# Attention and a mixture of soft slots on one core: q and k of four heads turned together, and combine's weights repeated for four results

## The chip, the cores and the metric

One Trainium2 chip, of which the kernel uses one core. The metric is the device time of one execution in microseconds (us). Three runs of the kernel before gave 297.88, 295.6 and 296.4 us; their median is 296.4. A profile was taken of one more execution, and all durations in this text come from it.

The engines by their names in the profile: PE is the matrix engine (PEld its weight loads), DVE the vector engine, ACT the scalar engine, POOL the general one, SP the one that here only issues transfers. POOL works through its instructions in order, and a transfer that it issues is one of them.

## The reference

Inputs: q, k, v of 8 batches, 12 heads, 448 tokens, 64 wide; phi (768 x 32); w1 and w2 of 8 experts (768 x 1024, 1024 x 768).

```python
scores = scale * np.matmul(q, k.transpose(0, 1, 3, 2))
m = np.max(scores, axis=-1, keepdims=True)
e = np.exp(scores - m)
attn = e / (np.sum(e, axis=-1, keepdims=True) + np.exp(-m) + 1e-09)
x = np.matmul(attn, v)             # then (batch * token, head * width) = 3584 x 768
...
logits = x @ phi
d = softmax of logits over the 3584 rows;  slot_input = d.T @ x
slot_out = relu(slot_input @ w1) @ w2        # four slots for each of the eight experts
c = softmax of logits over the 32 slots;   out = c @ slot_out
```

## The kernel before, in words

**Pairs and slots.** The 96 heads (8 batches of 12) are worked off as 48 pairs, six to a batch. `for s in range(3, NPAIR + 1)` (L769) goes over slots; a slot has two half-steps y = 0 and 1, and `hs = 2 * s + y` counts them. Slots 0 to 2 are written out by hand in `ramp` (L726). For slots 3 to 41 the work of each half-step is a string of words in `order` (L698), six rows, one for each value of s % 6. Slots 42 to 48 have no table.

**The words.** `T` turns q and k of pair s + 6: 28 transposes of 64x64 blocks on PE (L256, 7 token blocks, two heads, q and k), the two heads in two corners of the array, into one PSUM tile of 128x896, which one copy brings to SBUF (`T`, L241; on ACT in the ramp and for two of six pairs behind it, else on DVE). `B0` to `B3` (`Bk`, L352) make the scores of pair s, transposed, in four blocks of keys; a second matmul adds the negative row maxima, and ACT takes the exponential. Between them stand the score matmuls of a pair some three further on (`A`, L274), for the row maxima on DVE; the letters behind B give the order of these six matmuls. `V0` to `V3` and `H` (`AV`, L418) multiply by v; `H` does the last 64 queries, with 128x64 matmuls. `N` (`N1`, L440) brings the result to SBUF on ACT, `M` (`N2`, L449) divides it on POOL and writes it into `xb`, the x of the batch. `X` (`PX`, L491) turns 128 columns of x for the logits and copies them with ACT. `W` turns the maxima of a group of three pairs; `W1` (L310) prepares that on POOL. `P` runs the parts of the soft slots that are due at this half-step (`post`, L660).

**Shapes on PE.** Scores are 64x128 matmuls (two at once in the two halves of the rows), `B3` and its `A` and `T` are 64x64, `H` is 128x64, all else is 128x128.

**Loads.** Everything but the late rows of w2 is loaded by POOL, in order, with a cast to bf16. q and k come for three pairs at a time (`load`, L168, L176) into two buffers `nq0`, `nq1`; v for six heads (L180, L181) into one buffer `nv`, from which POOL copies it into `vp` (`V`, L403). `slot_loads` (L712) issues these: q and k at s % 3 == 2, `V` and the next v at s % 3 == 0. The weights' halves 0 to 10 (L843 to L851, `half_at`) have memory of their own. Halves 11 to 15 (40 rows of w2) lie over the buffers of the attention, and are loaded as these come free: `rows_at` (L694) says up to which row by which half-step. Rows 16 to 23 and 27 to 39 are first staged in DRAM as bf16 (`stage_at`, L696) and fetched by SP (L154).

**The end.** Behind the loop come the last logits, `hidden` (L887), `turn` (L903) and `slots` (L912), which leaves four partial sums of slot_out, one for each block of 32 partitions, in `so`. `select` (L941) adds the four and repeats the sum in four row blocks, by a matmul with `spread`, a matrix that POOL makes at L868 to L872. `result` (L957) multiplies 32 rows of c with one such block; `early` (L962) does a few results of one half of the columns, scales them on ACT and DVE, and `send` (L974) writes them out. `keep_busy` (L484) gives PE idle matmuls.

Of the kernel before, what the change touches and what calls it, by code (L numbers as in the profile page):

```python
# [24 lines left out]
HG = 6  # L25
NP = 3
# [5 lines left out]
def kernel(  # L32
# [47 lines left out]
    NQK, NE, VPN, NATV = 7, 5, HG * 4 * VS, HG * 4 * D  # L80
    sizes = [("nq0", 2 * NP * S), ("nq1", 2 * NP * S), ("nv", NATV), ("qk6", 2 * S), ("wm1", 512),
             ("qk0", 2 * S), ("qk1", 2 * S), ("qk2", 2 * S), ("wm0", 512), ("xTa", 4 * 512), ("qk3", 2 * S),
             ("vp0", VPN), ("x0", 4 * DD), ("qk4", 2 * S), ("qk5", 2 * S), ("e2", NE * 2 * S), ("e1", S),
             ("vp1", VPN), ("xTb", 2 * 512), ("x1", 4 * DD)]
# [72 lines left out]
    with ExitStack() as at:  # L157
# [9 lines left out]

        def load(g, nm, l0=0, l1=NP):  # L168
# [4 lines left out]
            if nm != "v":  # L173
                t = part(f"nq{g % 2}", "qk".index(nm) * NP * S, NP * S).rearrange("p (l x) -> p l x", l=NP)
# [10 lines left out]
        raw = w_tile(10)[:, 0:4 * S].bitcast(F32).rearrange("p (a x) -> p a x", a=2)  # L185
        for a, src in enumerate((q, k)):
            nc.sync.dma_start(out=raw[:, a, :], in_=src[0, 0:2].rearrange("h (j t) d -> (h j) (t d)", t=7))
# [26 lines left out]
        first_qk = [part(f"nq0", a * NP * S, NP * S).rearrange("p (l x) -> p l x", l=NP)[:, 0, :] for a in range(2)]  # L214
        nc.scalar.copy(first_qk[0], raw[:, 0, :])  # L215
        nc.vector.tensor_copy(first_qk[1][:, 0:4 * D], raw[:, 1, 0:4 * D])
        nc.scalar.copy(first_qk[1][:, 4 * D:S], raw[:, 1, 4 * D:S])
# [23 lines left out]
        def T(n):  # L241
# [5 lines left out]
            for a in range(2):  # L247
                src = nat["qk"[a], g]
# [3 lines left out]
                for tok, hl in order:  # L252
# [3 lines left out]
                    nc.tensor.transpose(o, src[r, pl, tok * D:(tok + 1) * D], ident[r, r])  # L256
# [11 lines left out]


# [132 lines left out]

        def V(g):  # L403
            t, s = vp[g % 2], nat["v", g]
            nc.gpsimd.tensor_copy(t[:, 0:HG:2, 0:3, 0:D], s[:, 0:HG:2, 1:4, :])
# [43 lines left out]
        def N2(n):  # L449
# [10 lines left out]
            else:  # L460
# [3 lines left out]
            c = pb * 128  # L464
            rec2 = psm.tile([128, 2], F32, tag="rec2", name="rec2", bufs=3)
            eng.tensor_mul(  # L466
                x[:, 0:3, c:c + 128].rearrange("p i (h d) -> p i h d", h=2),
                u[:, 0:6, 0:D].rearrange("p (i h) d -> p i h d", h=2),
                rec[:, 0:6].rearrange("p (i h) -> p i h", h=2).unsqueeze(3).to_broadcast([128, 3, 2, D]))
            if n == NPAIR - 1:  # L470
# [7 lines left out]
                x[:, 3, c:c + 128].rearrange("p (h d) -> p h d", h=2),  # L478
# [34 lines left out]
        def P(b):  # L513
# [7 lines left out]
            def l_mm(js):  # L521
# [13 lines left out]
                for j in js:  # L535
# [5 lines left out]
                    if b == B - 1:  # L541
# [5 lines left out]
                        if j == KC - 1:  # L547
                            l_turn()
                            keep_busy(2)
# [109 lines left out]

        post = {}  # L660
# [15 lines left out]
        for z in range(3):  # L676
            post.setdefault(2 * NPAIR - 5 + 2 * z, []).append(last[z])
# [11 lines left out]
        for _ in range(22):  # L689
# [4 lines left out]
        rows_at = {77: 3, 83: 7, 85: 12, 89: 17, 91: 20, 92: 24, 93: 26, 95: 27}  # L694
# [15 lines left out]
        wait_loads = []  # L710
        waits = [r for z in stage_at.values() for y in z for r in range(*y)]
        def slot_loads(s):  # L712
            g = (s + 10) // 3
# [352 lines left out]
```

## Time and profile before

| | |
|---|---|
| median of three runs | 296.4 us (295.6 to 297.88) |
| time of the profiled execution | 295.49 us |
| its span, first to last instruction | 293.7 us |
| PE busy in the span | 270.2 us |
| DVE, ACT, POOL busy | 249.7, 249.0, 196.3 us |
| six pairs in the body, from 107.87 to 136.50 | 28.63 us |
| HBM read and written | 89.16 MB, 15.14 MB |
| last fetch of weights lands | 257.33 us |
| first results sent, last ones landed | 263.69 us, 292.76 us |

A line of the page's groups, of a timeline or of a window is read like this: the line number in the kernel, the engine, the operation, what it writes and what it reads (W is the one big tile in SBUF, ps_ names are PSUM), partitions x elements and type, how many. In a timeline the first two numbers are the start in the span and the time until the last of the group ended; matmuls overlap, so that what one costs is read from start to start. A busy time near the length of the stretch says that the engine was never without work, not that it worked at its peak.

### The profile page before, as it was taken

What the parts mean: (1) busy time and instruction counts of PE and PEld (TensorE: products, weight loads), DVE (VectorE), ACT (ScalarE), POOL (GpSimd) and SP (SyncE); (2) the same over time, 40 slices, a digit from 0 to 9 for tenths busy, and PEclk for the clock granted to TensorE, in tenths of its full rate; (3) what the DMA queues carried; (4) which work ended last, traced back from release to release, by engine and by line L of the source; (5) the groups of instructions that cost most, each with busy time, mean ns of one, the idle gap of its engine ahead of it and who ended that gap; (6) DMA issues with size and microseconds to landing.
All of it is one profiled execution on the core that took longest, in us unless ns stands there. A gap on an engine that the chain in (4) does not pass through costs nothing.

```text
span 293.7 us, 12399 instructions
## 1 busy us (share of the span) xinstructions
PE 270.2 (92%) x5174; PEld 156.9 (53%) x5174; DVE 249.7 (85%) x581; ACT 249.0 (85%) x559; POOL 196.3 (67%) x391
## 2 busy tenths in 40 slices
PE   5999999999999999999999999999999999995810
PEld 4445555565665566565655665556555556652100
DVE  5999799999999989999999999999999565537920
ACT  4569999999999999999999999999999986337810
POOL 8786677889787978897888879887975823000000
PEclk9999999999999999999999999999999999999555
DMA  7999997999999999999999999999989999809997
GB/s 134 150 148 196 175 145 121 196 185 187 187 192 163 199 177 205 180 193 186 198 176 194 188 185 177 191 181 199 155 132 208 197 210 274 303 4 345 382 444 328
DMA packets 47016, 58.67 MB, mean 200 GB/s; under 512 B 2801, under 2 KB 39921, under 8 KB 46705
## 3 DMA queue, kind: packets, MB, share of 16 engines
q0 software_dynamic: 40304, 42.29, 90.7%
q1 hardware_dynamic: 6656, 15.60, 14.0%
q8 instruction: 40, 0.66, 0.8%
q14 instruction: 16, 0.12, 0.1%
HBM read 89.16 MB, written 15.14 MB: 355 GB/s over the span
## 4 chain that ended last, share of the span: by engine, by line
PE 77%; ACT 8%; DVE 4%; POOL 3%; issue 2%; DMA 1%; DVEq 0%; POOLq 0%; ACTq 0%
PE ps_av L433 16%; PE ps_b L367 10%; PE ps_a L285 10%; PE ps_t L256 8%; PE ps_b L370 7%; PE ps_b L393 4%; PE ps_x L498 4%; PE ps_b L396 3%; ACT W L399 2%; PE ps_s L620 2%; PE ps_o L959 2%; DVE mx L298 2%; PE ps_h L896 2%; PE ps_l L532 2%; PE ps_a L294 2%
## 5 line engine op out<-in xcount | busy, mean ns | idle before, releaser
L287 DVE TENSOR_REDUCE mx<-ps_a 128x1 f32<-128x448 f32 x250 | 139.1, 611 | 3.2 <-PE ps_a L285 2.4
L372 ACT ACTIVATE W<-ps_b 128x448 bf16<-128x448 f32 x250 | 125.0, 576 | 4.1 <-PE ps_b L370 3.3
L285 PE MATMUL ps_a<-W 64*128 64x448 bf16 x250 | 82.7, 354 | 0.0
L433 PEld LDWEIGHTS <-W 128*128 128x128 bf16 (+1 forms) x1536 | 53.9, 100 | 34.9 <-issue 31.1
L433 PE MATMUL ps_av<-W 128*128 128x65 bf16 (+1 forms) x1536 | 70.7, 196 | 0.6 <-ACT ubuf L446 0.6
L367 PE MATMUL ps_b<-W 64*128 64x448 bf16 x250 | 65.8, 355 | 0.0
L370 PE MATMUL ps_b<-mT,sel 64*128 64x448 bf16 x250 | 64.6, 350 | 0.0
L466 POOL TENSOR_TENSOR W<-ubuf,rec 128x384 bf16<-128x384 f32 x44 | 36.5, 829 | 27.5 <-DVE rec L462 14.5
L399 ACT ACTIVATE W<-ps_b 128x448 bf16<-128x448 f32 x86 | 46.5, 580 | 2.3 <-PE ps_b L396 2.0
L256 PEld LDWEIGHTS <-W 64*64 64x64 bf16 x1344 | 26.7, 112 | 17.5 <-issue 14.7
L256 PE MATMUL ps_t<-ident,W 64*64 64x64 bf16 x1330 | 31.2, 197 | 1.4 <-ACT W L215 1.4
L504 ACT CAST W<-ps_x 128x512 bf16<-128x512 f32 x47 | 29.6, 631 | 1.2 <-PE ps_x L498 1.0
L307 DVE TENSOR_REDUCE mx<-ps_a 128x1 f32<-128x448 f32 x48 | 29.6, 616 | 0.6 <-PE ps_a L304 0.6
L114 POOL DMA_DIRECT2D W<-in_moe_w_dram x30 | 22.7, 756 | 7.9 <-PE ps_b L396 7.7
L393 PE MATMUL ps_b<-W 64*64 64x448 bf16 (+1 forms) x134 | 26.8, 368 | 0.3
L285 PEld LDWEIGHTS <-W 64*128 64x128 bf16 x250 | 22.5, 94 | 7.8
L396 PE MATMUL ps_b<-mT,sel 64*64 64x448 bf16 (+1 forms) x134 | 25.4, 357 | 0.1
L370 PEld LDWEIGHTS <-sel 64*128 64x128 bf16 x250 | 20.7, 94 | 8.0 <-issue 2.7
L446 ACT COPY ubuf<-ps_av 128x455 f32<-128x455 f32 x44 | 24.4, 555 | 0.0
L263 ACT COPY W<-ps_t 128x896 bf16<-128x896 bf16 x21 | 19.7, 939 | 5.5 <-PE ps_t L256 5.5
L298 DVE TENSOR_REDUCE mx<-ps_a 128x1 f32<-128x448 f32 x38 | 21.1, 616 | 1.5 <-PE ps_a L294 1.5
L477 POOL TENSOR_TENSOR W<-ubuf,rec 128x128 bf16<-128x128 f32 x44 | 17.5, 398 | 3.7
(156 smaller groups left out, 446.6 us busy)
## 6 DMA issues: line engine op xcount, KB each, us to landing
W<-in_moe_w_dram POOLq DMA_DIRECT2D x24, 768.0 KB, 9.4
W<-in_v_dram POOLq DMA_DIRECT2D x32, 192.0 KB, 6.7
out_dram<-W SPq DMA_DIRECT2D x2, 2688.0 KB, 10.5
W<-in_q_dram POOLq DMA_DIRECT2D x15, 336.0 KB, 6.4
W<-in_k_dram POOLq DMA_DIRECT2D x15, 336.0 KB, 7.2
stage<-in_moe_w_dram POOLq DMA_DIRECT2D x4, 768.0 KB, 9.4
W<-stage SPq DMA_DIRECT2D x4, 576.0 KB, 6.9
out_dram<-W SPq DMA_DIRECT2D x6, 384.0 KB, 3.1
```

What stands on the lines that cost most here:

```text
L256: nc.tensor.transpose(o, src[r, pl, tok * D:(tok + 1) * D], ident[r, r])
L285: nc.tensor.matmul(ps[:, 0:S], t[r, 0, i * 128:(i + 1) * 128], t[r, 1, :], start=True, stop=True)
L287: nc.vector.reduce_max(m[:, c:c + 1], ps[:, 0:S], axis=AX.X)
L307: nc.vector.reduce_max(mx[g][:, c:c + 1], ps[:, 0:S], axis=AX.X)
L367: nc.tensor.matmul(pss[hl][:, 0:S], t[rs[hl], 1, cols], t[rs[hl], 0, :], start=True, stop=False)
L370: nc.tensor.matmul(pss[hl][:, 0:S], sel[rs[hl], 2 * pl + hl:2 * pl + hl + 1].to_broadcast([64, 128]), mT[mg(n)][rs[hl], :], start=False, s ...
L372: nc.scalar.activation(e[:, hl, :], pss[hl][:, 0:S], AF.Exp, scale=scale)
L393: nc.tensor.matmul(outs[hl], t[rs[hl], 1, cols], t[rs[hl], 0, :], start=True, stop=False)
L396: nc.tensor.matmul(outs[hl], sel[rs[hl], 2 * pl + hl:2 * pl + hl + 1].to_broadcast([64, m]), mT[mg(n)][rs[hl], :], start=False, stop=True)
L399: nc.scalar.activation(e, p[:, 0:S], AF.Exp, scale=scale)
L433: nc.tensor.matmul(o, eT[n, i, hl][:, qc], vp[g % 2][:, 2 * pl + hl, i, 0:W65], start=(i == 0 and u == 0 and hl == 0) or (u == 3 and i == ...
L466: eng.tensor_mul(x[:, 0:3, c:c + 128].rearrange("p i (h d) -> p i h d", h=2), u[:, 0:6, 0:D].rearrange("p (i h) d -> p i h d", h=2), rec[: ...
```

## The change

**Turning.** The buffers `nq0` and `nq1` become one, `raw`, with room for four times two heads of q and of k. `load4(j)` loads q and k of four heads (pairs 2j and 2j + 1), half of `raw`. `T4(j, a)` turns q (a = 0) or k (a = 1) of these four heads: 14 transposes, each with 128 partitions and 64 columns in and 64 partitions by two runs of 64 columns out, for heads 2l and 2l + 1 at once; one copy of 128x896 brings them to the buffers of two pairs. A pair is then made of heads 0 and 2, or 1 and 3, of its four. So `N2` writes to two columns of heads that are not neighbours, `PX` has to wait for both pairs of four and comes at s - 3, and `V` sorts v into other places of the two `vp` buffers. The first six pairs and the last two are turned as before. There are eight buffers of turned q and k in place of seven.

**Orders.** The word `T` is replaced by `Q` and `K`, three of each in six slots; all six rows of `order` are new, and the ramp, which turns pairs 6 and 7 with `Q3.0` and `Q3.1`, turns no pair 8 and has no `PX(0)`. Loads of v, `V`, the halves of weights and the staging move by half-steps; as the buffers lie elsewhere, `rows_at` is new.

**Combine.** `repeat(z)` multiplies `spread` with 32 rows of c, so that the weights of a result stand in all four row blocks (`cR`). Four results of the first half (t = 0, 1, 4, 5 of the first two batches) are then one matmul of 128 rows each with `so` itself, and go ahead of `select`. `repeat(1)` takes the place of `keep_busy(2)` in the last logits, `repeat(0)` stands before PX(47) with `keep_busy(2)` instead of 4. Two more results of the second two batches are made as half rows.

```diff
-    NQK, NE, VPN, NATV = 7, 5, HG * 4 * VS, HG * 4 * D
...
+    NQK, NE, VPN, NATV = 8, 5, HG * 4 * VS, HG * 4 * D
+    sizes = [("raw", 8 * S), ("nv", NATV), ("wm1", 512)] + [(f"qk{i}", 2 * S) for i in range(6)] + \
+            [("wm0", 512), ("xTa", 4 * 512), ("x0", 4 * DD), ("qk6", 2 * S), ("qk7", 2 * S), ("free", 2 * S),
+             ("e2", NE * 2 * S), ("e1", S), ("vp0", VPN), ("vp1", VPN), ("xTb", 2 * 512), ("x1", 4 * DD)]
...
+        four = lambda n: PB <= n < NPAIR - 2
+
+        def load4(j):
+            b, m = divmod(j, 3)
+            for a, x in enumerate((q, k)):
+                x = x[b, 4 * m:4 * m + 4].rearrange("(l h) (j t) d -> (h j) l (t d)", h=2, t=7)
+                gdma(out=raw[a][:, 2 * (j % 2):2 * (j % 2) + 2], in_=x)
...
+        def T4(j, a):
+            n = 2 * j
+            turned[j] = turned.get(j, 0) + 1
+            if j > 3 and turned[j] == 2 and j + 2 < NPAIR // 2:
+                wanted.append(j + 2)
+            if not four(n):
+                T(n + a)
+                return
+            ps = psB.tile([128, 2, S], BF16, tag="b", name="ps_t")
+            for tok in range(7):
+                for l in range(2):
+                    c = kcol(l, tok) if a else (2 * tok if tok < 4 else 2 * tok - 7) * 64
+                    nc.tensor.transpose(ps[64 * l:64 * l + 64, :, c:c + 64], raw[a][:, (n + l) % 4, tok * D:(tok + 1) * D],
+                                        ident)
+            cp = nc.scalar.copy if (n + a) % 6 in (0, 3) else nc.vector.tensor_copy
+            o = at_[f"qk{n % NQK}"] + a * S
+            cp(R[:, o:o + 4 * S].rearrange("p (h x) -> p h x", h=2)[:, :, 0:S], ps)
...
+        def repeat(z):
+
+            ps = pb_("ps_rep")[:, 0:256].rearrange("p (t c) -> p t c", t=2)
+            r = slice(32 * z, 32 * z + NS)
+            for h in range(2):
+                nc.tensor.matmul(ps[:, h, :], spread[r].rearrange("p r s -> p (r s)"),
+                                 cT[r, 0, h, :, :].rearrange("p b j -> p (b j)"), start=True, stop=True)
+            t = psm.tile([128, S], BF16, tag="mT", name="cR")[:, 0:256].rearrange("p (t c) -> p t c", t=2)
+            (nc.scalar.copy if z else nc.vector.tensor_copy)(t, ps)
+            cR.append(t)
...
-        rows_at = {77: 3, 83: 7, 85: 12, 89: 17, 91: 20, 92: 24, 93: 26, 95: 27}
+        rows_at = {79: 1, 85: 4, 88: 12, 89: 13, 91: 17, 92: 21, 93: 22, 95: 25}
...
-        order = (("P V2 B0assbba V3 B1sabsba",
-                  "H N B2ssbaba T B3 P V0 V1 X M"),
-                 ("V2 P B0assbba V3 B1saasbb",
-                  "H P N B2assbba T B3 V0 V1 X M"),
-                 ("V2 B0assbba P V3 B1assbba",
-                  "H N B2asasbb B3 T W P V0 V1 M X"),
-                 ("B0assbba P V2 V3 H N B1ssabba T",
-                  "M B2sasbba B3 X V0 P V1"),
-                 ("B0assbba T B1sasbba P V2 V3 H",
-                  "N B2assbab B3 V0 P M X V1"),
-                 ("B0assbba V2 V3 P B1sabsab H N",
-                  "B2ssbaab T B3 P V0 W V1 M X"))
...
+        order = (("V2 V3 B0sasbab H N P B1asbsab",
+                  "Q M X P B2assbba V0 V1 B3"),
+                 ("B0assbba V2 V3 P B1asbsab H K N",
+                  "P B2sabsab B3 V0 V1 M X"),
+                 ("V2 X B0assbba B1asbsab V3 P",
+                  "H N B2assbba P V0 W M V1 B3"),
+                 ("B0sabsba B1asbsab V2 P V3",
+                  "H N K M Q B2sabsab P V0 V1 B3 X"),
+                 ("B0assbba V2 B1asbsab P V3 H Q",
+                  "N B2assbba X P V0 V1 B3 M"),
+                 ("B0assbba V2 V3 B1asbsab P H K",
+                  "N B2sabsab B3 M P V0 W V1 X"))
...
-                "A B1.0 A K0 Y2 K1 D0 V0.3 H0 C1.1 N0 B1.2 A T6 C1.3 V1.0 V1.1 A B2.0 M0 A T7 B2.1 A V1.2 V1.3 W2 T8 "
-                "H1 A N1 B2.2 V2.0 X2 C2.3 Z0 V2.1 M1 K2 ")
...
+                "A B1.0 A K0 Y2 L4 D0 V0.3 H0 C1.1 N0 B1.2 A Q3.0 C1.3 V1.0 V1.1 A B2.0 M0 A Q3.1 B2.1 A V1.2 V1.3 W2 "
+                "H1 A N1 B2.2 V2.0 X2 C2.3 V2.1 M1 L5 ")
...
+                c = s % 6
+                if (c, y) in ((1, 0), (4, 0)) and (s + 2) // 3 < NG:
+                    V((s + 2) // 3)
+                if y == 0:
+                    if s % 3 == 2 and s + 1 in firsts:
+                        W1(mg(s + 1))
+                    if c % 3 == 2 and (s + 4) // 3 < NG:
+                        load((s + 4) // 3, "v")
+                while wanted:
+                    load4(wanted.pop())
...
+            if half == 0 and bp == 0 and t in (0, 1, 4, 5):
+                nc.tensor.matmul(ps, cR[t % 4][:, t // 4, :], so[:, halfs[0]], start=True, stop=True)
+                return
...
         slots(0, range(3), [1])
+        early([(0, 0), (0, 1)], 0)
+        send(0, 0, 2, halfs[0])
+        slots(0, range(3, 5), [1])
+        early([(0, 4), (0, 5)], 0)
         select(0)
...
+        slots(1, range(6, FK), [1])
+        nc.scalar.copy(so[:, halfs[1]], pss[1][:, 0:ND])
+        early([(1, 4), (1, 5)], 0, 1)
+        send(1, 4, 6, halfs[0])
         select(1)
```

More of the change, by code (lines that the diff above doesn't have):

```diff
@@ L213 @@
         nc.vector.memset(ones[64:128, 1:2], 0.0)
[L214 to L217, printed above, removed]
+        nc.scalar.copy(raw[0][:, 0, :], f32[:, 0, :])
+        nc.vector.tensor_copy(raw[1][:, 0, 0:4 * D], f32[:, 1, 0:4 * D])
+        nc.scalar.copy(raw[1][:, 0, 4 * D:S], f32[:, 1, 4 * D:S])
         for h in range(2):
@@ L255, in T @@
                     o = k0[c // 256][r, 0, c:c + 64] if a and n == 0 else ps[r, a, c:c + 64]
[L256 removed]
+                    nc.tensor.transpose(o, src[r, n - NP if NP <= n < PB else n % 4, tok * D:(tok + 1) * D], ident[r, r])
             t = qk_t[n % NQK]
@@ L755 @@
             elif op == "J":
-                for nm in "qk":
-                    load(2, nm)
+                load4(3)
                 load_half(0, 0, w_tile(0))
+            elif op == "Q":
+                T4(*arg)
+            elif op == "L":
+                load4(*arg)
             elif op == "D":
@@ L821 @@
                                 AV(s, i, range(3))
+                    if hs in px_at:
+                        PX(px_at[hs])
                     for f in post.get(hs, ()):
                         f()
-                    if y and 0 <= s - 2 < NPAIR - 2:
-                        PX(s - 2)
+                    if y and s == NPAIR - 3:
+                        nc.gpsimd.memset(xb[1][0:64, 3, 10 * D:11 * D], 0.0)
                     if y == 0:
@@ L877 @@
         last[3]()
-        keep_busy(4)
+        repeat(0)
+        keep_busy(2)
         PX(NPAIR - 1)
@@ L960, in result, with early @@
                              start=True, stop=True)
-        def early(bp, ts, half, act=0):
+        def early(rows, half, act=0):
             pss_ = []
-            for t in ts:
+            for _ in rows:
                 st["out"] = st.get("out", -1) + 1
@@ L1023 @@
                 pss = [psO.tile([128, 2, 512], F32, tag="o", name="ps_o") for _ in ts]
-                hfs = range(int(bp == 1 and t0 < 4), 2)
+                hfs = range(int(bp == 1 and t0 < 6), 2)
                 for hf in hfs:
```

131 lines of the change are left out of this document (61 added, 70 removed).

## The prediction

> **What bounds the kernel now.** I read the page first: the engines' shares, then the chain that ended last, then the DMA queues.
>
> ```profile
> PE 270.2 (92%) x5174; PEld 156.9 (53%) x5174; DVE 249.7 (85%) x581; ACT 249.0 (85%) x559; POOL 196.3 (67%) x391
> PE 77%; ACT 8%; DVE 4%; POOL 3%; issue 2%; DMA 1%; DVEq 0%; POOLq 0%; ACTq 0%
> W<-in_v_dram POOLq DMA_DIRECT2D x32, 192.0 KB, 6.7
> ```
>
> PE carries 77% of the chain, DMA 1%. An average hides the stages, so the table of stretches came next; its columns are stretch, PE, PEld, DVE, ACT and POOL busy, granted clock, DMA share, GB/s.
>
> ```profile
> 23.00:33.00 10.00, 9.38 (x188) 5.24 (x185) 8.75 (x20) 9.79 (x22) 4.88 (x11) 1.00 1.23 202
> 107.87:136.50 28.63, 28.63 (x597) 17.32 (x595) 27.70 (x64) 27.93 (x66) 24.36 (x47) 1.00 1.16 191
> 216.00:220.00 4.00, 4.00 (x77) 2.22 (x75) 3.96 (x11) 4.00 (x12) 2.46 (x7) 1.00 0.58 76
> 264.00:276.00 12.00, 8.29 (x69) 2.50 (x62) 9.82 (x16) 9.05 (x16) 0.00 (x0) 0.77 0.95 344
> 276.00:292.00 16.00, 3.53 (x15) 0.54 (x12) 4.55 (x5) 3.77 (x5) 0.00 (x0) 0.50 1.02 430
> ```
>
> Four regimes. The ramp's second half (23 to 33) is ACT's: 9.79 of 10 us. In the body, six pairs take 28.63 us and PE never rests; ACT (27.93) and DVE (27.70) are within 1 us of it, POOL has 4.3 us to spare, and the DMA share (1.16, where 1 is 16 engines without overlap) says that the loads run nearly without a gap. Behind 276 the results go out at 430 GB/s and no engine matters. So the change can win in the ramp on ACT, in the body only on PE's own stream, and in the tail only by writing sooner.
>
> Next the timeline of PE in the body, for what a turn costs:
>
> ```profile
> 72.32 0.57 PE L256 MATMUL ps_t<-ident,W 64*64 64x64 bf16 x24
> 72.70 0.38 PE L304 MATMUL ps_a<-W 64*64 64x448 bf16 x2
> 72.72 0.23 PE L256 MATMUL ps_t<-ident,W 64*64 64x64 bf16 x4
> 72.79 0.36 PE L393 MATMUL ps_b<-W 64*64 64x448 bf16 x2
> ...
> 75.97 0.32 PE L433 MATMUL ps_av<-W 128*64 128x65 bf16 x8
> 76.22 0.36 PE L367 MATMUL ps_b<-W 64*128 64x448 bf16 x2
> ```
>
> The reader is to see that 28 small transposes take 0.46 us from first start to the next work (14 pairs of 29 ns; both 64x64 corners run at once), and that the eight AV matmuls of shape 128x64 take 0.25 us, 0.09 of it the gap before another shape starts: four pairs of 40 ns, so the two column halves run at once too.
>
> Last, the ramp on ACT and the tail on PE:
>
> ```profile
> 27.57 0.91 ACT L263 COPY W<-ps_t 128x896 bf16<-128x896 bf16 x1
> 29.21 0.95 ACT L263 COPY W<-ps_t 128x896 bf16<-128x896 bf16 x1
> 32.34 0.69 ACT L504 CAST W<-ps_x 128x512 bf16<-128x512 f32 x1
> ```
>
> ```profile
> 261.74 0.33 PE L944 MATMUL ps_sel<-W,ubuf 128*128 128x192 bf16 x2
> 261.99 0.67 PE L916 MATMUL ps_so<-W 128*32 128x384 bf16 x12
> 262.60 0.34 PE L959 MATMUL ps_o<-W,cT 32*128 32x384 bf16 x2
> ```
>
> **Part by part.** All against the profiled execution: span 293.7, its time 295.49 us, which is 0.9 below the median of the three runs (296.4; 295.6 to 297.88).
>
> *Ramp (before slot 3).* T7 and T8 no longer copy on ACT: one goes to DVE (the key half of pairs 6 and 7), one moves into slot 3. PX(0) moves out too. From start to next start on ACT those took 0.79, 0.79 and 0.46 us: 2.0 us out of an engine that runs without rest. PE loses T8 (28.49 to 29.05, 0.56 us) and PX(0) (31.63 to 31.86, 0.23), and had an idle 0.62 at 30.66: it allows 1.4. DVE gains one copy of 0.53 (L265's 0.62, less its overlap) and had idle 0.48 and 0.64 us there, and 0.43 just behind: it allows about 1.0. What is late next is therefore DVE. Bounds 0.5 to 1.4; I take 1.0, DVE's.
>
> *Turning in the body.* A T4 issues 14 transposes of 128x64 with 128 columns moving, two column halves at once. No such transpose is in the trace. The nearest row is PX, whose four matmuls also stream 128 columns and take 0.23 us (245.88 to 246.11), 56 to 57 ns each. Lower bound: the halves overlap, seven of these, 0.40 us. Upper: they don't, 14 of these, 0.79. I take 0.40, as the AV row of the same shape overlaps. Six T before also stream 14 times 28.5 ns, 0.40 each: turning itself wins nothing. What moves is the change of array shape, 0.09 us each by the gap above. Counting shapes through the old six rows of orders gives 44 changes in six pairs, through the new ones 43: five of six T4 stand beside the 128x64 AV of the same slot (H K, H Q), but B3 now stands alone. One change less and 0.01 us less per turn: 0.15 us in six pairs, bounds 0 and 0.4 (a T beside B3 cost 0.44, one alone 0.56, a T4 beside H 0.40, less two changes that the other words gain). Over 39 slots, 6.5 times: 1.0 us.
>
> [...]
>
> *Copies, loads, V.* ACT and DVE keep two and four copies of 128x896 in six pairs; that the output has a stride between two runs of 448 I cost at nothing. POOL's q and k loads go from four (0.77 to 0.83 us) to six of two thirds the size; single ones took 0.55, so about 0.66: 4.0 for 3.2 us, 0.8 us more in six pairs, covered by POOL's 4.3 us of rest. Behind a load4 that waits for its T4 stand N2 and the next V; x is read one slot later than before (PX at s-3), which covers a few us. Bytes are the same. V does the same four copies, but two pairs (9.6 us) after its load is issued instead of three; v landed 6.3 to 7.7 us behind its issue. Cost 0; without the cover, see the third rival. The half-step moves of the weights' halves and of the staging queue behind these on POOL and meet no reader before the end.
>
> *End of the body (slots 39 to 48).* The turn put off is made there (slot 39 turns q and k): +0.4. One PX more falls into the last slots: 0.23 of PE: +0.2, bounds 0 and 0.5.
>
> *Repeat.* Two matmuls of 128 columns and a copy of 128x256, twice. repeat(1) takes the place of eight small idle matmuls beside a DVE reduction (0.29); repeat(0) waits for POOL's first row of spread, which is now behind a load of rows 25 and 26 that waits for an AV of the last pair. Before, the memset began at 244.89 and PX(47) at 247.11; now I put spread's first part at about 247.2. +0.1, bounds 0 and 0.7.
>
> *Tail.* The first two results no longer wait for select and its copies (261.74 to 262.60): PE reaches them 0.86 sooner, but they are two full matmuls of 163 ns in turn; the first send goes about 0.75 us sooner. Two tiles more leave as half rows; at 344 to 368 GB/s against 430 that costs 0.3 us for 0.79 MB, some of it in gaps. -0.6, bounds -0.9 and 0.
>
> *Last weights.* Rows 1 to 15 come later by memory that frees later: four rows issued by the end of slot 42 where ten were. The loads before had half a gap at 216 to 220 (share 0.58) and at 232 to 236. From slot 41 on I add up one v (2.1 us), eight staged rows at 0.95, 18 direct ones at 1.08 and 21 fetches at 0.58, all from landings before: 41.3 us from 215.6, end near 257; before, the last landed at 257.33 and the last rows are read at 260.5. 0, bounds 0 and +2.5.
>
> Sum: -1.0 -1.0 +0.4 +0.2 +0.1 -0.6 = -1.9, from 295.49 to 293.6; from the median, 296.4 to 294.5.
>
> **Rivals.**
> 1. *More of everything.* Ramp 1.4, body 0.4 in six pairs (2.6), tail 0.9, end +0.4: -4.5, 291.9. For it: the stretch 78.70 to 107.87 is 0.5 us longer than its neighbours and a POOL wait stands in its chain, which a later PX could remove. Against: ACT and DVE are 0.7 and 0.9 us behind PE and take over soon. 0.22.
> 2. *Late weights.* The queue idles around slot 40, where little is issued; slots(1) then waits for the last fetched rows. Each us beyond 260.5 less the 2 us won counts whole: +1 to +2.5, about 296.2. 0.13.
> 3. *POOL late (slower).* If v lands over about 13 us behind its issue (9.6, and some 4 us that V and the N2 behind it have), V stops POOL, N2 frees ubuf late, ACT's N1 and PE wait. Half a us for each of 14 V is +7: 301.5. For: POOL goes from 85% to 88%, and a weight half before took up to 12.1 us to land. Against: no v took over 7.7. 0.10.
> 4. *Halves in turn.* If T4's column halves don't overlap, 0.79 for 0.40, 40 times: +16, 310.5. If its weight loads (110 ns in L256's rows) stand between the pairs as well, seven times 0.167: +31, 325. [...] Against: the 40 ns pairs. 0.05.
>
> **How the numbers follow.** Forecast 0.50, rivals 0.22, 0.13, 0.10, 0.05. The likeliest gives 294.5. The forecast's bounds are 292.8 to 296.4. The range leaves out rival 4, nearly all of rival 3 and the lower end of rival 1: 291.8 to 298.8. One per cent, about what a measurement of this kernel tells from no change, is 293.4 and 299.4: faster takes rival 1 and the low end of the forecast, 0.28; slower rivals 3 and 4, 0.15; the same 0.57.
>
> **What would show it.** Turning: T4's 14 matmuls in about 0.40 us, two starting at once; wrong if single ones follow each other at 55 ns. Ramp: the first matmul of the mixed kind (L367 before) near 31.1 instead of 32.14, and on ACT one copy of ps_t between T5's and slot 3's, not three. Body: six pairs in 28.4 to 28.6 us. POOL: no idle time ended by a landing of v. Tail: the first send 0.75 us closer behind the copy of so, and nothing of slots(1) waiting for a fetch. The prediction is wrong if the body's period grows, or if the last landing passes the first read of its row.

## The result, and the profile after

The changed kernel takes 297.8 us (median of 20 runs, 296.96 to 299.45), the kernel before beside it 296.84 (20 runs, 295.6 to 298.48): a ratio of 1.0042 [1.0025, 1.0059]. That is within 1%, in the range, and on the wrong side: 1.9 us of gain were forecast, 1.2 us were lost (1.0 by the medians). Each ratio and its interval here are an estimate from the runs of both kernels that were not in the chip's slower state, not the quotient of the two medians. The profiled execution took 296.96 us, its span is 295.1, against 295.49 and 293.7.

The page of the changed kernel, in the rows shown of the one before:

```profile
span 295.1 us, 11242 instructions
PE 269.5 (91%) x4602; PEld 154.2 (52%) x4602; DVE 252.0 (85%) x585; ACT 249.4 (84%) x559; POOL 206.0 (70%) x408
PE 73%; ACT 7%; DVE 6%; DMA 3%; POOL 3%; issue 3%; DVEq 0%; POOLq 0%; ACTq 0%
W<-in_v_dram POOLq DMA_DIRECT2D x32, 192.0 KB, 6.2
```

PE has 572 matmuls fewer and is busy 0.7 us less in a span that is 1.4 longer. The table of stretches shows no stage that went wrong as a whole (columns as before):

```profile
23.00:33.00 10.00, 9.82 (x138) 5.07 (x137) 9.79 (x22) 8.86 (x21) 6.11 (x13) 1.00 1.18 192
107.87:136.50 28.63, 28.63 (x513) 16.98 (x513) 27.91 (x65) 28.27 (x67) 26.28 (x50) 1.00 1.18 191
216.00:220.00 4.00, 4.00 (x64) 2.16 (x62) 3.97 (x10) 3.91 (x11) 3.35 (x8) 1.00 0.57 68
264.00:276.00 12.00, 8.35 (x79) 2.32 (x73) 9.76 (x17) 8.56 (x18) 0.00 (x0) 0.81 0.98 350
276.00:292.00 16.00, 4.11 (x17) 0.70 (x15) 5.13 (x6) 4.36 (x5) 0.00 (x0) 0.50 1.03 425
292.00:296.00 4.00, 0.00 (x0) 0.00 (x0) 0.00 (x0) 0.00 (x0) 0.00 (x0) 0.50 0.01 5
```

The ramp is now DVE's (9.79 of 10, ACT 8.86). In the body ACT has come within 0.36 us of PE. The queue still has its gap at 216 to 220. Behind 292, when the kernel before has all but landed, a DMA share of 0.01 lasts on.

So the loss has to be found mark by mark. I took the same events from both traces (starts of the slots, the last N1, the last matmul of PX(47), the copy of the first slot result to `so`, the last landing, the end of the span). The entries are the time that a stretch takes, less what it takes in the kernel before, in us:

| from mark to mark | forecast | changed | `spread_first` | `mended` | `mended_split` |
|---|---|---|---|---|---|
| start to slot 3 | -1.0 | -0.09 | -0.54 | -0.41 | -0.42 |
| slot 3 to 39 | -1.0 | -1.19 | -1.19 | -1.21 | -1.20 |
| slot 39 to 40 (turn put off) | +0.4 | +0.49 | +0.50 | +0.51 | +0.50 |
| slot 40 to the last N1 | +0.2 | +0.41 | +0.41 | +0.41 | +0.42 |
| last N1 to PX(47) | +0.1 | +0.83 | +0.31 | +0.31 | +0.31 |
| PX(47) to copy of `so` | 0 | 0.00 | +1.54 | +0.19 | 0.00 |
| copy of `so` to last landing | -0.6 | +0.67 | +0.69 | -0.46 | -0.46 |
| last landing to end of span | none | +0.35 | +0.35 | +0.35 | +0.01 |
| sum | -1.9 | +1.47 | +2.06 | -0.32 | -0.84 |

The last three columns are experiments, told below. The body gives what was forecast. The gain is lost in three places behind it: 0.83 before PX(47), 1.3 us between forecast and fact in the tail, and 0.35 behind the last landing, for which the forecast had no term.

**Before PX(47).** The chain of waits of the changed kernel (start, us, what):

```profile
245.22 0.49 ACT W L556
245.71 0.60 issue
246.31 0.04 POOL W L113
246.34 0.48 issue
246.83 0.23 POOL ubuf L924
247.06 0.04 issue
247.10 0.03 POOLq L927
247.13 0.00 issue
247.13 0.32 POOL ubuf L927
247.45 0.05 issue
247.50 0.28 PE ps_rep L719 x2
247.78 0.34 PE ps_idle L541 x8
248.12 0.22 PE ps_x L550 x4
```

POOL waits, issues the load of rows 25 and 26 (L113), clears `spread` (L924), writes its first row (L927); only then can repeat(0) run, and PX(47) stands behind it. The chain names ACT's copy of PX(45) as what POOL waited for, but that had ended at 245.70. POOL's wait names PE's semaphore too, and its record ends at 245.82, just behind an AV matmul of the last pair (245.78), in this profile and in three others alike. In the kernel before, PX(47) followed ACT's last scaling for pair 47 (L474), and POOL was not in the chain:

```profile
247.30 0.32 ACT W L474
247.62 0.05 issue
247.66 0.24 PE ps_x L498
```

The timeline of POOL of the changed kernel says how long it had nothing else to do (its last entry names ACT for the same reason):

```profile
246.31 0.53 POOL L113 DMA_DIRECT2D W<-in_moe_w_dram  x1 [9.83 <-ACT W L556]
```

Two constants, whose memory had come free at 240.6 (there they begin where they are put first, below), were queued behind a load that waited 9.83 us.

**The tail.** The queues of the stretch 264 to 296, first of the kernel before, then of the changed one; the GB/s row has 40 slices of 0.8 us:

```profile
GB/s 84 346 355 371 357 374 359 361 369 346 382 348 369 371 369 424 407 403 396 522 430 430 430 430 430 430 430 430 430 430 430 430 430 430 430 0 0 0 0 0
q1 hardware_dynamic: 3536, 11.01, 87.1%
```

```profile
GB/s 219 357 361 351 357 359 369 367 348 376 355 361 385 315 376 371 376 378 401 499 426 430 430 430 430 457 430 430 430 430 430 430 430 430 430 27 0 0 0 0
q1 hardware_dynamic: 3920, 11.01, 88.0%
q8 instruction: 1, 0.02, 0.2%
```

Both write at 430 GB/s to the 35th slice. Then the changed kernel has one slice at 27, a sixteenth of 430, which is what one engine of sixteen would move. And a queue shows up that the kernel before does not have in this stretch: one packet of 16,384 bytes, "instruction", that the records put at 274.16 and 0.93 us. Of the sixteen last packets of the output, 4 bytes each, fifteen end at 292.2 to 292.4 and one at 293.56; before, all sixteen end at 292.2 to 292.4. I take the packets of this queue for fetches of PE's program, as their number goes with its length: 40 of them over 10,348 matmuls and weight loads before (twice 5174), 36 over 9,204 after, one for 259 and for 256. Before, the last came at 263.42, ahead of the first send (263.69).

**Behind the last landing.** SP closes with waits on the eight semaphores that its transfers use in turn (48 landings on each before, 64 on s101 and s102 after), in both traces in the same order. The trace's records of SP (start, semaphore), before and after:

```
before   286.39 s117   292.78 s118                                   (last landing 292.76)
after    287.54 s101   293.90 s102   293.96 s113   294.02 s114
         294.08 s115   294.14 s116   294.20 s117   294.26 s118       (last landing 293.88)
```

With 24 transfers the last one's semaphore is waited for last; with the 26 of the changed kernel (two more fetches of staged rows) it is second, and six waits of 0.06 us still follow.

### The profile page after: what moved, and what is told of

The parts are those of the page before. It is cut to its first block, busy times and chain, and to the rows that moved or that the text cites. A ratio compares the mean times of both kernels' runs of the same rounds, so it can differ in the third digit from the quotient of the medians.

```text
span 295.1 us, 11242 instructions
## 1 busy us (share of the span) xinstructions
PE 269.5 (91%) x4602; PEld 154.2 (52%) x4602; DVE 252.0 (85%) x585; ACT 249.4 (84%) x559; POOL 206.0 (70%) x408
## 4 chain that ended last, share of the span: by engine, by line
PE 73%; ACT 7%; DVE 6%; DMA 3%; POOL 3%; issue 3%; DVEq 0%; POOLq 0%; ACTq 0%
PE ps_av L482 16%; PE ps_a L317 11%; PE ps_b L399 8%; PE ps_b L402 7%; PE ps_b L425 5%; PE ps_t L294 5%; PE ps_x L550 4%; DMA W<-in_k_dram 3%; PE ps_b L428 3%; DVE mx L330 2%; ACT W L431 2%; PE ps_s L672 2%; PE ps_h L953 2%; PE ps_o L1019 2%; ACT W L404 2%
## 5 line engine op out<-in xcount | busy, mean ns | idle before, releaser
L404 ACT ACTIVATE W<-ps_b 128x448 bf16<-128x448 f32 x250 | 122.4, 569 | 2.3 <-PE ps_b L402 0.8
L317 PE MATMUL ps_a<-W 64*128 64x448 bf16 x250 | 86.2, 353 | 0.1
L402 PE MATMUL ps_b<-mT,sel 64*128 64x448 bf16 x250 | 69.0, 350 | 0.0
L399 PE MATMUL ps_b<-W 64*128 64x448 bf16 x250 | 68.8, 354 | 0.1
L431 ACT ACTIVATE W<-ps_b 128x448 bf16<-128x448 f32 x86 | 45.1, 564 | 4.0 <-PE ps_b L428 3.9
L317 PEld LDWEIGHTS <-W 64*128 64x128 bf16 x250 | 23.3, 93 | 14.8 <-issue 5.4
L113 POOL DMA_DIRECT2D W<-in_moe_w_dram x30 | 22.7, 756 | 10.0 <-ACT W L556 9.8
L556 ACT CAST W<-ps_x 128x512 bf16<-128x512 f32 x47 | 28.3, 616 | 0.6 <-PE ps_x L550 0.6
L402 PEld LDWEIGHTS <-sel 64*128 64x128 bf16 x250 | 23.3, 95 | 10.4 <-issue 4.1
L294 PE MATMUL ps_t<-ident,W 128*64 128x128 bf16 x560 | 21.3, 220 | 0.0
L1012 DVE TENSOR_SCALAR W<-ps_o,ubuf 128x384 f32<-128x384 f32 (+1 forms) x21 | 15.3, 766 | 5.3 <-PE ps_o L1016 2.8
L451 POOL COPY W<-W 128x384 bf16<-128x384 bf16 (+1 forms) x29 | 18.9, 652 | 0.9
```

Source lines behind the costliest of these rows:

```text
L294: nc.tensor.transpose(ps[64 * l:64 * l + 64, :, c:c + 64], raw[a][:, (n + l) % 4, tok * D:(tok + 1) * D], ident)
L317: nc.tensor.matmul(ps[:, 0:S], t[r, 0, i * 128:(i + 1) * 128], t[r, 1, :], start=True, stop=True)
L399: nc.tensor.matmul(pss[hl][:, 0:S], t[rs[hl], 1, cols], t[rs[hl], 0, :], start=True, stop=False)
L402: nc.tensor.matmul(pss[hl][:, 0:S], sel[rs[hl], 2 * pl + hl:2 * pl + hl + 1].to_broadcast([64, 128]), mT[mg(n)][rs[hl], :], start=False, s ...
L404: nc.scalar.activation(e[:, hl, :], pss[hl][:, 0:S], AF.Exp, scale=scale)
L431: nc.scalar.activation(e, p[:, 0:S], AF.Exp, scale=scale)
```

## The experiments

Theories for the loss: A, the late `spread` before PX(47); B, the last weights as a second wall right behind it; F, the fetch of program between the sends. Rivals: S, the first loads, which landed later in the changed kernel's profile (k of pairs 3 to 5 at 15.29 us, before at 14.35); T, the new order of the tail itself. All kernels but `combine_undone`, `combine_alone`, `turn_clean` and `before_fetch_late` hold the whole change.

**The change again.** `after_again` is the changed kernel unaltered.

> The changed kernel as it is, once more, for a second profile. Theory A (the loss is spread's late matrix, 0.8 us, and later PX in the last slots, 0.3): the same ratio, 1.003 to 1.005; PX(47) again behind POOL's row of spread, and the start of slot 0 and the last DMA engine's end free to move. Rival S (the early loads land later because of where they go): k of pairs 3 to 5 lands near 15.3 us again, not 14.35, and slot 1 starts near 21.8. Rival T (the new tail makes one DMA engine late): the last result lands over 1 us behind most engines again.

297.65 us against 296.82, ratio 1.003 [1.0011, 1.0049]. k of pairs 3 to 5 landed at 13.31, ahead of the kernel before, and the loss stayed: S is out, and the -0.09 of the table's first row is partly this chance (-0.48 here). The profile showed a new cost: 40 idle matmuls between two parts of the soft slots took 2.13 us here, 1.18 in the changed kernel's first profile. First the chain of `after_again`, then of the changed kernel:

```profile
249.62 2.13 PE ps_idle L541 x40
```

```profile
249.87 1.18 PE ps_idle L541 x40
```

The granted clock was 0.5 for 3.41 us there (248.56 to 251.97). The same happened in `combine_alone` (250.27 to 253.68), and at this place in no profile of a kernel that has all its idle matmuls (`keep_busy`) near PX(47).

**The spread first.**

```diff
-        load_rows(rows, 35)
         nc.gpsimd.memset(spread, 0.0)
...
+        load_rows(rows, 35)
         last[3]()
         repeat(0)
```

> The changed kernel with spread and own4 made on POOL ahead of the last rows' loads, not behind them. Theory A: repeat(0) no longer waits, PX(47) starts near 247.3 in place of 248.12, ratio to before about 0.8 us lower than the changed kernel's, 1.000 to 1.002. Rivals S and T: no change in the time beyond noise, 1.003 to 1.005, as PX(47) would wait for something else.

297.1 us, ratio 1.0014 [0.9992, 1.0036]. PX(47) comes at 247.15, 0.51 ahead of the kernel before: A holds, worth 0.52 (0.83 less 0.31). But the next wall stands 0.5 us behind. The chain of this kernel:

```profile
252.13 0.05 issue
252.18 0.03 SPq L153
252.21 0.03 issue
252.24 9.27 DMA W<-stage
261.50 0.04 issue
261.55 0.48 PE ps_so L973 x5
```

and its waits (engine and line, who ended them: us, times, longest):

```profile
PE ps_so L973 <- DMA W<-stage: 1.1, 1, 1.1
```

The last fetched rows land at 261.50 (before: 257.33), and PE waits 1.1 us for them: B holds. In the changed kernel they landed at 260.86, just before PE came for them; A had hidden B.

**One half of the change at a time.** `combine_undone` is the changed kernel with the old combine; `combine_alone` the kernel before with repeat and the new order of results:

```diff
-                            repeat(1)
+                            keep_busy(2)
...
-        repeat(0)
-        keep_busy(2)
+        keep_busy(4)
...
-            if half == 0 and bp == 0 and t in (0, 1, 4, 5):
-                nc.tensor.matmul(ps, cR[t % 4][:, t // 4, :], so[:, halfs[0]], start=True, stop=True)
-                return
...
```

> The changed kernel with the combine part undone: no repeat, the idle matmuls as before, select ahead of the first results, and the order of results as before. Theory A: it wins the 0.8 us of spread and loses the 0.4 that the earlier first send is worth, so about 0.4 us faster than the changed kernel, ratio 1.001 to 1.003. Rival T: it wins 1.5 to 2 us, ratio 0.997 to 0.999. Rival S: as the changed kernel, within 0.3 us.

> The kernel before with the combine part alone (repeat, the new order of results); turning, loads and orders as before. Here the matrix spread is made at 244.9 to 246.7, so that repeat(0) does not wait. Theory A: faster by 0.4 us, ratio 0.998 to 0.999. Rival T: slower by 0.7 to 1.2 us, ratio 1.002 to 1.004. Rival S: the ratio is 1.000 or a little under, and all of the loss is in the other part.

`combine_undone`: 297.52 us, 1.0028 [1.0011, 1.0045], so the turning alone is as slow as the whole: the ratio is one that A gave, but A's 0.4 us of gain are not there (297.65 for the change again). Its last weights land at 261.45 and a fetch of program lies in its tail too (269.95), 32.31 us from the copy of `so` to the last landing against 31.55 before: T is out, as this is the old order. `combine_alone`: 296.92 us, 1.0019 [0.9996, 1.0041], unclear, and above the 0.998 to 0.999 that A gave; its profile holds that stretch at half clock (1.18 us more from PX(47) to the copy of `so`) and a fetch at 268.5, and still the tail is 0.12 us shorter. From the last N1 to PX(47) it takes 0.00 more than before: repeat(0) is free where POOL has `spread` in time.

**Rows earlier.** `spread_rows` is `spread_first` with the last eight staged rows a slot earlier and rows 1 to 3, 7 and 8 loaded some half-steps earlier:

```diff
-        rows_at = {79: 1, 85: 4, 88: 12, 89: 13, 91: 17, 92: 21, 93: 22, 95: 25}
+        rows_at = {79: 1, 83: 4, 88: 12, 89: 13, 91: 17, 92: 21, 93: 22, 95: 25}
...
-        stage_at = {34: [(16, 20), (20, 24)], 37: [(27, 29), (29, 32)], 40: [(32, 36), (36, 40)]}
+        stage_at = {34: [(16, 20), (20, 24)], 37: [(27, 29), (29, 32)], 39: [(32, 36), (36, 40)]}
...
+            if 2 * s + 1 == 85:
+                load_rows(7, 9)
...
```

> The changed kernel with spread made early, as in the run before, and with the late rows of w2 issued sooner: the last eight staged rows one slot earlier, rows 1 to 3 at the end of slot 41 in place of 42, rows 7 and 8 at the end of slot 42. Theory B (the weights are the wall behind the matrix spread: with spread early, slots waited 1.5 us for the last fetch, which landed at 261.5): the last fetch lands near 258, the time from the first hidden matmul to the copy of so falls from 11.5 to 9.9 us, ratio 0.996 to 0.999. Rival F (a DMA engine that fetches PE's program in the tail ends last): the copy of so may come sooner, but the last result still lands 0.8 us behind the other engines. Rival G (the total of the loads is the wall, whatever the order): the last fetch lands at 260 or later, and the ratio stays at 1.001.

296.52 us against 297.27, ratio 0.9973 [0.9948, 0.9998]. The last rows land at 260.32, 1.18 sooner, and the copy of `so` is 0.13 us behind the kernel before instead of 1.02. The landing near 258 that B gave was missed (G gave 260 or later), but the ratio is B's and not G's. The tail is as in the changed kernel: 32.22 us, with a fetch at 273.83.

**The fetch moved, both ways.** `fetch_early` is the changed kernel with 64 idle matmuls more in the ramp (26 at its start and twice 19), 128 instructions of PE, so that the last fetch falls ahead of the sends; `before_fetch_late` the kernel before with 78, so that one falls among them:

```diff
-        for _ in range(22):
...
+        pad(22 + 26)
...
-        ramp = ("T0 A A T1 A A W0 T2 A G0 A X0 J0 A B0.0 ...
+        ramp = ("T0 A A I19 T1 A A W0 I19 T2 A G0 A X0 J0 A B0.0 ...
...
+            elif op == "I":
+                pad(*arg)
...
```

> The changed kernel with 64 more idle matmuls in the ramp, where PE waits for its first loads: 128 more instructions, so that the last 16 KB of PE's program are fetched near 262 us, before the first result is sent, in place of 274. Rival F: no DMA engine ends 0.8 us behind the others, and the ratio falls by 0.6 to 0.8 us, from 1.003 to about 1.001. Theory B: unchanged within 0.3 us. If the idle matmuls cost something, slot 3 starts later than 31.7.

> The kernel before with 78 more idle matmuls in the ramp: 156 more instructions, which moves a fetch of 16 KB of PE's program from just before the first send (263.4) into the time when all DMA engines write results (near 270). Rival F: one engine ends about 0.8 us behind the rest and the ratio is 1.002 to 1.003, with nothing else changed. Theory B: ratio 1.000.

`fetch_early`: 297.63 us, ratio 1.000 [0.9966, 1.0035], the runs far apart (295.11 to 300.0). In its profile the fetches lie at 259.1 and 263.1, the straggler is gone, and from the copy of `so` to the last landing it takes 31.09 us against 32.22: F holds, 1.13 us. The time alone does not show it. `before_fetch_late`: 300.11 us, 1.0079 [1.0047, 1.0112], where 1.002 to 1.003 was forecast. This was a poor test: in its profile the idle matmuls made slot 3 start 3.19 us late. Read by the tail alone, a fetch at 272.3 took it from 31.55 to 32.05, half a us.

**All of it mended.** `mended` has the spread first, the rows as in `spread_rows`, the idle matmuls of `fetch_early`, and `keep_busy` beside both repeats. `mended_again` is the same kernel; `mended_bare` leaves out all idle matmuls that were added, which makes it the kernel of `spread_rows`, line for line; `turn_clean` takes out the part on combine; `busy_back` is the changed kernel with the 16 idle matmuls beside the repeats and nothing else.

> The changed kernel with all of it: spread early, rows early, 64 more idle matmuls in the ramp, and the idle matmuls that repeat had replaced put back beside it (the granted clock fell to half for 3.4 us near 249 in two profiles without them). If spread 0.8, late weights, the fetch 0.8 and the clock are what the change lost: ratio 0.990 to 0.994, the clock at 1.00 until the tail. If the loss lies elsewhere (the loads in sum, the tail's order): 0.998 or more.

> The mended version once more, unchanged, to narrow its interval. Theory (the turning is worth about 1 us by the end of the body; the late spread, the late last weights, the late fetch of program behind the sends and the missing idle matmuls had eaten it): 0.995 of the kernel before, 0.993 to 0.997, 295.4 us against 296.9; in its trace the output lands 31.1 us behind the copy of the first result, as in the first run of it. If the first run was luck of the chip: 0.998 to 1.002.

> The mended version without any of the added idle matmuls (none in the ramp, none beside the repeats), which brings the fetch of the last piece of the program back behind the first sends. If that fetch is what the end lost: the output lands 32.2 us behind the copy of the first result in place of 31.1, the copy itself stays where it was (261.0 to 261.3), and the time is 0.9 to 1.3 us above the mended version of this call. If the fetch does not matter and the mended version won by other means: within 0.3 us of it. If the idle matmuls matter through the clock alone: the same landing behind the copy, but a stretch at half clock near 250 us in some runs, 0.2 to 0.4 us in the mean.

> The mended version with the part on the weights of combine undone (no repeats, the old order of the results), so the turning by pairs alone with the mended loads and idle matmuls. If the new order at the end is worth what the traces show once no fetch lies in it (31.55 against 31.09 us behind the copy): 0.4 us slower than the mended version, less the 0.2 us that the second repeat adds ahead of the last weight multiplication: 0.2 to 0.5 us slower. If the part on combine is what made the change slow: faster than the mended version by 0.5 us or more.

> The changed kernel with sixteen idle matmuls put back beside the two repeats and nothing else. If the half clock near 250 us that some profiled runs showed comes of their absence: no run with a mean clock under 0.95, where 4 of 20 runs of the changed kernel had one, and 0.2 to 0.4 us faster than its 1.003 to 1.004 of the kernel before, so 1.002 to 1.003; the loss through the late spread and the late fetch stays. If the dip is a matter of the chip: 1.003 to 1.004, with such runs among them.

| kernel | median | beside it, before | ratio | copy of `so` to last landing | last fetch of program |
|---|---|---|---|---|---|
| `mended` | 295.6 | 297.27 | 0.995 [0.9919, 0.9981] | 31.09 | 261.59 |
| `mended_again` | 294.95 | 296.68 | 0.9962 [0.9929, 0.9995] | 31.10 | 261.2 |
| `mended_bare` | 296.81 | 296.68 | 0.9992 [0.997, 1.0014] | 32.13 | 274.36 |
| `turn_clean` | 295.62 | 296.68 | 0.9992 [0.9964, 1.0021] | 31.52 | 264.76 |
| `busy_back` | 296.76 | 296.68 | 1.0003 [0.9988, 1.0018] | 31.46 | 268.48 |

The mended kernel beats both, if by less than the 0.990 to 0.994 that was forecast. The table's ratios go by all runs of a kernel, so `turn_clean`, with five of twelve runs at 297.16 us or more and the rest at 295.16 to 295.75, has a low median and no gain in its ratio. Without the idle matmuls its fetch is back at 274.36 and so is the straggler: the queues of 264 to 296, `mended` and then `mended_bare`:

```profile
GB/s 359 373 326 361 365 365 369 350 371 371 359 369 336 378 371 374 371 398 595 430 430 430 430 430 430 430 430 430 430 430 430 430 430 430 0 0 0 0 0 0
```

```profile
GB/s 344 380 332 374 353 371 357 371 348 376 357 365 353 353 361 378 374 386 701 428 415 457 403 403 430 430 430 430 430 430 430 430 430 430 108 27 0 0 0 0
q8 instruction: 1, 0.02, 0.2%
```

That is 1.03 us more in the tail, and 0.3 to 0.4% in the ratio, where the intervals still overlap. The same kernel as `spread_rows` had 0.9973 and has 0.9992 here, so what it gains on the kernel before is not clear of noise. `turn_clean` against `mended`: the new order of results is worth 0.43 us in the tail, where 0.6 was forecast. `busy_back` was expected to keep its late fetch; it did not. Its 32 instructions more brought the fetch from 274.16 to 268.48 and the tail from 32.22 to 31.46, so its better ratio is F's more than the clock's. No run of it had a mean clock under 0.956, where 4 of 20 of the changed kernel had 0.946; how much of the time that is worth stays open, as both effects move in one edit. The four took 298.97 us in the mean and the other sixteen 297.64, which is 0.27 us in the mean of all 20: about so much of the loss goes with the lowest clock, whatever its cause.

The profiled execution of `turn_clean` has slot 3 two us late and was 2.2 us over the kernel's median. The chain in the ramp, `mended` and then `turn_clean`:

```profile
6.32 0.66 PE ps_idle L758 x19
6.98 0.56 PE ps_t L268 x28
7.54 0.34 PE ps_a L326 x2
```

```profile
6.55 1.12 PE ps_idle L757 x19
7.67 0.88 PE ps_t L268 x14
8.55 0.53 PE ps_a L326 x2
```

The same words of the ramp, each 1.6 to 1.7 times as long. The records of the granted clock begin 5.85 us into the span of `mended` and 14.32 us into that of `turn_clean`, and about up to its first record `mended` is as slow: two matmuls of ps_a take 0.53 us at 5.48 and 0.34 at 7.54. So the idle matmuls that move the fetch cost nothing in the profile whose records begin early, and about 2 us in the one whose records begin late. I take this to be why the runs of the padded kernels lie so far apart; runs without a profile do not show it. Nor did the early records give `mended` the fastest ramp: its slot 3 starts 0.41 us before that of the kernel before, those of `spread_first` and `spread_rows`, whose records begin at 14.28 and 13.17, 0.54 and 0.55.

**The closing waits.** `mended_split` is `mended` with 32 transfers on SP in place of 26:

```diff
+                n = 1 if hi - lo == 3 and r1 < 40 else hi - lo
+                for j in range(0, hi - lo, n):
+                    nc.sync.dma_start(out=W[:, o + j * DD:o + (j + n) * DD].rearrange("p (j f) -> p j f", f=DD),
+                                      in_=t[:, lo - a + j:lo - a + j + n, :])
```

> The mended version with three of SP's fetches of three rows each cut into single rows: 32 transfers by SP in place of 26 (24 in the kernel before), bytes and times of issue otherwise the same. SP's semaphores for transfers go round by eight, and the waits at the end go through them in a fixed order; with 24 transfers the last one's is waited for last, with 26 second, so that six waits of 0.06 us follow it. If that is where 0.34 us between the last landing and the end of the span went (0.92 before, 1.26 in the changed kernel and in the mended one): 0.90 to 0.95 here, and the time 0.3 us under the mended version's, 294.6 to 295.0, as far as the fetches land no later. If the 0.34 us are due to something else in the new kernel: 1.26 again.

From the last landing to the end of the span it takes 0.93 us (before 0.92, `mended` 1.26): shown. 294.59 us against 296.92, ratio 0.9951 [0.9923, 0.998]; its profile is the shortest of the study:

```profile
span 292.8 us, 11416 instructions
PE 270.5 (92%) x4682; PEld 155.8 (53%) x4682; DVE 251.6 (86%) x585; ACT 249.4 (85%) x559; POOL 207.1 (71%) x410
```

From the changed kernel to this one the table's sum falls by 2.31 us: 0.52 by `spread`, 1.13 by the fetch, 0.34 by the closing waits, and 0.33 in the ramp, by which profiles of the same ramp differ too (-0.09 and -0.48 above). The late weights do not show in this sum, as they were hidden in the changed kernel.

## Why the prediction was wrong

Three steps failed: repeat was priced at +0.1 and cost 0.52; the tail's sum had no term for a fetch of program among the sends, which cost 1.13; and the closing waits, 0.35, had no term at all.

*Turning in the body: right.* T4's two column halves run at once: in the trace of the changed kernel the 14 transposes from 71.83 on start in pairs, the two 2 to 3 ns apart, and a pair 54 to 56 ns behind the one before. The timeline of PE:

```profile
71.67 0.32 PE L482 MATMUL ps_av<-W 128*64 128x65 bf16 x8
71.83 0.56 PE L294 MATMUL ps_t<-ident,W 128*64 128x128 bf16 x14
72.31 0.36 PE L399 MATMUL ps_b<-W 64*128 64x448 bf16 x1
```

Fourteen transposes are over in 0.48 us with the change of shape, and two T4 in succession take 0.39 each in the chain: the lower bound of 0.40. Six pairs take 28.46 to 28.78 us where they took 28.62 to 29.17; slot 3 to 39 gains 1.19 for 1.0. Rival 4, whose T4 took 0.79 us or more, did not come.

*Ramp: mechanism right, gain three quarters.* From slot 1 to 3 the changed kernel gains 0.78 and DVE is the new bound, as worked out. What is left at slot 3 is less, as slot 1 came 0.69 us later in this profile. It came 0.21 later in `combine_alone` as well, whose ramp is that of the kernel before, and in no other profile did it come before 21.33 (here 21.12): part of it is an early start in the one profile of the kernel before.

*The turn put off and the last slots.* +0.49 for +0.4; +0.41 for +0.2, within its bounds. But another +0.31 to +0.40 between the last N1 and PX(47) belongs to the turning as well: it stands in `turn_clean`, which has no repeat.

*Repeat: the chain was cut short.* "Now I put spread's first part at about 247.2": its row began at 247.13, as put, and behind an AV of the last pair, as put. What failed is the price, +0.1, where 0.52 of the table's 0.83 are repeat's (inside the bounds of 0 to 0.7): I set that start against PX(47)'s own, 247.11, and left out what stands between the two: the row itself 0.32, repeat 0.28, idle matmuls 0.34. Added up from 247.2 they put PX(47) at 248.1, which is where it was. Where `spread` is ready, repeat(0) costs nothing (`combine_alone`).

*Last weights: right only by accident.* "End near 257" was 260.86. The sum of 41.3 us counted each transfer's time, and not that the gap at 216 to 220 (share 0.57) stayed and that rows wait for memory. The term was 0 because A delayed PE by as much; with A mended it was +1.54. Rival 2, at 0.13, describes what the runs show once A is mended; in the changed kernel itself nothing waited for the last fetch.

*Tail: -0.6 became +0.67.* The first send is 0.74 us closer behind the copy of `so` (1.75 us for 2.49; forecast 0.75), and the order is worth 0.46 where no fetch disturbs it. What the sum had was right in kind; it lacked a term. The page of the kernel before has the row "q8 instruction: 40, 0.66, 0.8%", and I passed over it as too small. What counted here is not its share but where the last one fell, and the edits that changed PE's instruction count moved it: 128 more from 274.16 to 263.1 (`fetch_early`), 32 more to 268.48 (`busy_back`).

*POOL and V: right in the conclusion, short in size.* POOL went from 24.36 to 26.28 us in the stretch of the body, 1.9 us for the 0.8 worked out: the six loads of q and k take 0.71 to 0.77 us each and not 0.66, 4.4 for 4.0, and one piece of an N2 more falls into the stretch. Its rest covers that: v lands 6.2 us behind its issue in the median, and POOL waits for a landing of v once, 1.07 us in the ramp, and never in the body. Rival 3 did not come.

The sum misses by 3.4 us: tail 1.3, ramp 0.9, PX(47) 0.7, closing waits 0.35, slots 39 and on 0.3, less 0.2 that the body gained more. Most of it is in the last 50 us, where no engine is full and every mark hangs on one late event.

## What to carry to other kernels

When a change gives a late stage a new reader, follow the whole chain from that reader's source to the path, and ask what is queued ahead of the source on its engine; a constant belongs in front of every load that waits (here one waited 9.83 us, with `spread` behind it). When it changes the number of instructions or of transfers, look at where the last fetch of program falls against the final writes (1.13 us here), and which closing wait the last transfer has (0.34 us). And when one wait is mended, the next wall may be close behind it, here half a us: the time shows only the sum, the marks show both.

## What the runs showed of the hardware

- Packets of 16,384 bytes, queue "instruction": 40 over 10,348 matmuls and weight loads in the kernel before, 36 over 9,204 in the changed one, about one for 256. That they bring PE's program is inferred from this, and from the edits that moved them. With the last at 274.16, among the writes (changed kernel), one of the sixteen last packets of the output ended at 293.56, the others by 292.4; with the last at 263.42 (before) all ended by 292.4. By the tail's length against that of a kernel with the same order and no such packet, one cost 1.03 to 1.16 us when it came 12.5 to 13.0 us behind the copy of `so` (five traces), 0.76 and 0.50 at 7.8 and 7.5, 0.34 to 0.37 at 5.3 and 6.3. In the six traces with the fetch ahead of the sends, tails of the same order agree within 0.03 us. The records do not name engines: that the packet and the straggler share one is inferred.
- 40 idle matmuls took 1.17 to 1.18 us at a granted clock of 1.00, and 2.13 (`after_again`) and 2.02 (`combine_alone`) in a stretch of 3.41 us at 0.5; seen in two of the seven profiles of kernels with sixteen idle matmuls fewer just before, and in none of the eight with them.
- The closing waits of SP stood 0.06 us apart, and how many followed the last landing hung on the count of transfers: with 24 (before) and 32 (`mended_split`) the span ended 0.92 and 0.93 us behind the landing, with 26 (`mended`) 1.26. That the count goes by eight is read from the semaphores.
- Two column halves of 128x64 ran at once: a T4's 14 transposes of 128 columns took 0.39 us in the changed kernel.
